# Output products of two tiles begun inside the last attention rounds, with weights, constants and last channels loaded in another order

## The chip, the cores and the metric

One core of a Trainium2 chip runs the whole program. Its engines work side by side, each on its own list of instructions in a fixed order: PE (matrix products; its weight loads are listed as PEld), DVE and ACT (elementwise work, both read PSUM), POOL (elementwise work on SBUF) and SP, which here only issues DMAs. The metric is the device time of one execution in microseconds (us), as the median of some runs.

## The reference

The reference runs two kinds of layer in turn, twice: attention over a sliding window, then a spectral filter.

```python
def _A_ref(x, wqkv, wo):
    B, S, D = x.shape                       # 1, 2048, 576
    H = 32; Dh = D // H; W = 256            # 32 heads of 18
    qkv = (x @ wqkv).reshape(B, S, 3, H, Dh).transpose(2, 0, 3, 1, 4)
    q, k, v = qkv[0], qkv[1], qkv[2]
    scores = jnp.einsum("bhqd,bhkd->bhqk", q, k) * (Dh ** -0.5)
    ...  # causal mask, window of 256
    p = _softmax(scores, axis=-1)
    o = jnp.einsum("bhqk,bhkd->bhqd", p, v)
    return o.transpose(0, 2, 1, 3).reshape(B, S, D) @ wo
...
x = x + _A_ref(_layernorm(x, axis=-1), A_wqkv, A_wo)
x = x + _B_ref(_layernorm(x, axis=-1), B_w_r, B_w_i)   # rfft2, times W, irfft2
x = x + _A_ref(_layernorm(x, axis=-1), A_wqkv, A_wo)
x = x + _B_ref(_layernorm(x, axis=-1), B_w_r, B_w_i)
```

The change lies in the last part of each attention layer: the products with `wo`, and how they join the attention that comes before.

## The kernel before

`layer_a` works through the heads in 8 groups (n) of four heads, and through the tokens in 16 blocks (i) of 128. A round `t` of its loop runs from -10 (`-LEAD`) to 129 (`NX + 1`), with `NX` = 128 pairs of group and block. In a round stand, on PE in this order, twice (for `pair` 0 and 1): two E products (`exps`: keys against queries, of pair `t`, which ACT then exponentiates into `P`), two S products (`score_max`: of pair `t + 10`, whose row maxima DVE takes), and in pair 0 also the product of probabilities and values of pair `t - 2` (`pv`, sixteen small products into the bank `U`). POOL masks the `P` tiles. S products end with round 117, so rounds 118 to 127 have E products alone. Every fourth round `m_rows` turns the maxima (`tpm`) and `norm` turns and divides a finished chunk of 512 tokens (`tpo`), and stores it to DRAM: channels 0 to 447 to `o_d`, the last 128 to `o7_d`.

PSUM has eight banks. Here they are held as three of the tag S, two of E, two of pj and the bank `U`. The function `bank` hands them out in rotation, from the list `banks`: S, S, E, E, S while projections hold pj, and with the two pj banks in the list from round 103 on. A product into a bank waits until the reader of its last content is done; so in a list of n banks it waits for the reader of the n-th use before.

The output product goes by 16 tiles of 128 tokens (u; tile u holds every sixteenth token). Its channels come back from DRAM (`load`: 448 channels into `o`, and the tile of x beside it; `last`: the last 128 channels of all tiles into `o7`), are turned by PE (`turn`, `turn_last`) and split into a high and a low part by ACT, DVE and POOL. `early` makes the products of the first 448 channels, eleven steps of two halves (288 columns each); `late` makes the three steps of the last 128 channels, adds x on DVE and stores the tile. Tiles 0 to 2 have their early products right behind the loop, between the last transposes of attention (`tpz`, whose results go into `o7` without passing through DRAM); then come the late products of tiles 0 to 2, and from tile 3 on a pipeline that the spectral layer shares. `OB` is 120. The tiles of weights, constants (`dc`, `gc`) and channels lie in SBUF where the projections' inputs were, which are free from round 103 on.

No scheduler moves anything: the order on each engine is that of the code.

Of the kernel before, what the change touches and what calls it, by code (L numbers as in the profile page):

```python
# [8 lines left out]
F32 = mybir.dt.float32  # L9
F32R = mybir.dt.float32r  # L10
# [5 lines left out]
S, D = 2048, 576  # L16
DF = 289
NF = 290
# [409 lines left out]
NQ = 8  # L428
# [72 lines left out]
class Out:  # L501


    def __init__(self, nc, ident, eps, bp, ov, o7v, srcv, dstv, wo_d, dc_d, gc_d):
        self.__dict__.update(nc=nc, ident=ident, eps=eps, bp=bp, ov=ov, o7v=o7v, srcv=srcv, dstv=dstv, wo_d=wo_d, dc_d=dc_d, gc_d=gc_d)
        self.ps = {}

# [21 lines left out]
    def consts(self):  # L529

        self.dcs = []
        for k, t in enumerate(("wraw", "wraw", "wqh", "wqh", "wql")):
            d = self.bp.tile([128, 2, NF], F32R, tag=t, name=f"dc{k}", bufs=2)
            self.nc.sync.dma_start(d.bitcast(F32), self.dc_d[:, 2 * k:2 * k + 2].bitcast(F32))
            self.dcs.append(d)
        self.nc.sync.dma_start(self.gc.rearrange("p a c -> p (a c)").bitcast(F32), self.gc_d.bitcast(F32))

    def load(self, u):
        self.nc.sync.dma_start(self.o[u % 3], self.ov[:, u])
        self.nc.sync.dma_start(self.x[u % 5], self.srcv[:, u])  # L540
# [7 lines left out]
    def turn(self, u, tp, e, last=None):  # L548
# [11 lines left out]
        if last is not None:  # L560
            self.split_last(u, last)

    def turn_last(self, u, tp):
        self.nc.tensor.transpose(tp, self.o7[:, u], self.ident)
# [6 lines left out]

    def steps(self, u, ks, first, last):
        for i, (x, p, wk) in enumerate(ks):
            for n in range(2):
                self.nc.tensor.matmul(self.ps[u][n][:, 0:288], x, self.w[p][:, wk * D + n * 288:wk * D + n * 288 + 288],  # L575
                                      start=first and i == 0, stop=last and i == len(ks) - 1)

    def early(self, u, ps, some=slice(0, 11)):
# [10 lines left out]
        self.steps(u, ks[some], some.start == 0, False)  # L589

# [38 lines left out]
def layer_a(tc, src, dst, wqk_d, wv_d, wo_d, dc_d, gc_d, dram, copy, wvs, wos, second, spectral):  # L629
# [9 lines left out]
    with ExitStack() as ctx:  # L639
# [129 lines left out]
        with ExitStack() as c2:  # L769
# [55 lines left out]

            banks, later, stores = ["S", "S", "E", "E", "S"], [], []

# [133 lines left out]

            OB = NX - 8
            out = Out(nc, ident, eps, bp, ov, o7v, srcv, dstv, wos, dc_d, gc_d)

            for t in range(-LEAD, NX + 2):
# [58 lines left out]
                if t - OB - 3 in (0, 1, 2, 4):  # L1024
                    out.tail(min(t - OB - 3, 3))
                if t - OB - 5 in (0, 1, 2):
                    u = t - OB - 5
                    out.turn(u, pp.tile([128, 512], F32, tag="pj", name=f"tpa{u}", bufs=2), V)
                    if u < 2:
                        out.load(u + 3)  # L1030
# [5 lines left out]
            for k in range(4):  # L1036
                tp = pp.tile([128, 512], F32, tag="E" if k in (1, 2) else "pj", name=f"tpz{k}", bufs=2)[0:32]
                for a in range(4):
                    T.transpose(tp[:, 128 * a:128 * a + 128], us[NQ - 1, 3][:, 4 * k + a:512:16], ident)
                tv = tp.rearrange("p (a h e) -> p a h e", a=4, h=4)  # L1040
# [6 lines left out]
            tp = pp.tile([128, 512], F32, tag="pj", name="tpl", bufs=2)  # L1047
# [15 lines left out]
            out.turn(4, pp.tile([128, 512], F32, tag="E", name="tpa4", bufs=2), A)  # L1063
        spectral(dst, out.dcs, out.gc, ident, out.rh, out.rl, out)
# [30 lines left out]
```

## Time and profile before

| | |
|---|---|
| median of 3 runs | 1461.99 us (1460.09 to 1463.79) |
| profiled execution | 1459.43 us |
| its span | 1457.7 us |
| granted PE clock, mean | 0.975 |
| PE busy | 1362.7 us (93%) |
| DVE, ACT, POOL busy | 946.6, 809.0, 710.8 us |
| L575, the output products | 784 products, 113.8 us |
| loop of the first attention layer ends, its second | 481.12, 1205.85 us |

The busy time of PE is a sum of spans in which products overlap, so a stretch of time is better read from the starts of its instructions. In the order of time a row gives start, length, engine, line, operation, what it writes and reads, the shape and how many like it were merged; behind it, in brackets, how long the engine was idle before and what ended that.

### The profile page before, as it was taken

How to read it: one execution, taken by the hardware profiler on the slowest of the kernel's cores; microseconds unless marked ns; L12 is line 12 of the kernel's file. 1: busy time of each engine (PE TensorE's matmuls, PEld its weight loads, DVE VectorE, ACT ScalarE, POOL GpSimd, SP SyncE). 2: the span in 40 equal slices, each digit the busy share in tenths (PEclk: the TensorE clock that was granted, in tenths of full speed). 3: DMA queues.
4: the chain of work that ended last, by engine and by line, in shares of the span. 5: the costliest groups of instructions: out<-in, count | busy, mean ns of one | idle time of the engine just before them, and what ended most of it. 6: DMA issues, size and time to landing. Idle time of an engine off the chain costs nothing.

```text
span 1457.7 us, 35798 instructions
## 1 busy us (share of the span) xinstructions
PE 1362.7 (93%) x12536; PEld 1063.8 (73%) x12536; DVE 946.6 (65%) x3053; ACT 809.0 (56%) x1907; POOL 710.8 (49%) x1205
## 2 busy tenths in 40 slices
PE   7998999999999999887879999999999998998888
PEld 7987666666665889847879876666666657997478
DVE  4347778887776566564543487778877864565645
ACT  5622677667768344325545236776676683443255
POOL 2345556666655333153612555655555552431536
PEclk9999999999999999997989999999999999999979
DMA  7866455545546657686575575555454565576865
GB/s 231 263 184 221 152 168 176 172 156 176 161 144 174 191 183 220 201 246 207 202 237 123 162 227 165 161 155 157 137 153 142 162 182 162 186 225 200 238 215 193
DMA packets 198335, 269.93 MB, mean 185 GB/s; under 512 B 86988, under 2 KB 109068, under 8 KB 196940
## 3 DMA queue, kind: packets, MB, share of 16 engines
q1 hardware_dynamic: 188428, 251.04, 56.1%
q10 hardware_dynamic: 9216, 13.37, 2.9%
q0 software_dynamic: 512, 3.23, 0.8%
q8 instruction: 101, 1.65, 0.5%
q14 instruction: 78, 0.64, 0.1%
HBM read 166.34 MB, written 103.79 MB: 185 GB/s over the span
## 4 chain that ended last, share of the span: by engine, by line
PE 77%; DMA 10%; DVE 5%; ACT 4%; issue 2%; POOL 1%; SPq 1%; ACTq 0%; DVEq 0%; POOLq 0%
PE pj L803 14%; PE U L919 11%; PE S L871 9%; PE E L899 9%; PE vps L759 8%; PE ops L575 6%; PE po L216 3%; PE pf L216 3%; PE pi L401 2%; PE tpo L929 2%; DMA ofree<-yd 1%; ACT P L900 1%; DMA o_d<-o 1%; DMA qs<-mt 1%; PE pz L236 1%
## 5 line engine op out<-in xcount | busy, mean ns | idle before, releaser
L873 DVE CUSTOM_DVE_ANT_0 jk<-S,mask 128x384 bf16<-128x384 f32 (+2 forms) x1024 | 497.6, 529 | 94.9 <-PE S L871 90.2
L900 ACT ACTIVATE P<-E 128x384 f32<-128x384 f32 (+2 forms) x1024 | 422.2, 477 | 172.3 <-PE E L899 142.3
L902 POOL TENSOR_SCALAR_AFFINE_SELECT P<-P 128x512 f32<-128x512 f32 x256 | 162.3, 634 | 274.3 <-ACT P L900 262.7
L871 PE MATMUL S<-ks,qs 63*128 63x384 f32 (+2 forms) x1024 | 237.8, 365 | 3.4 <-ACT P L900 1.0
L899 PE MATMUL E<-qs,ks 64*128 64x384 f32 (+2 forms) x1024 | 220.9, 395 | 7.9 <-DMA qs<-mt 5.2
L919 PE MATMUL U<-P,vq 128*19 128x128 f32 (+1 forms) x3840 | 203.1, 330 | 2.5 <-POOL P L905 2.0
L899 PEld LDWEIGHTS E<-qs,ks 64*128 64x128 f32 x1024 | 119.1, 184 | 83.8 <-issue 32.5
L871 PEld LDWEIGHTS S<-ks,qs 63*128 63x128 f32 x1024 | 132.2, 185 | 50.0 <-ACT P L900 23.0
L803 PE MATMUL pj<-xh,wqh 64*128 64x512 f32 (+1 forms) x640 | 164.8, 403 | 2.1 <-ACT vt L763 1.7
L919 PEld LDWEIGHTS U<-P,vq 128*19 128x19 f32 x3840 | 90.1, 98 | 95.7 <-issue 34.4
L905 POOL TENSOR_SCALAR_AFFINE_SELECT P<-P 128x512 f32<-128x512 f32 x224 | 142.0, 634 | 0.0
L803 PE MATMUL pj<-xl,wqh 64*128 64x512 f32 (+1 forms) x512 | 127.8, 393 | 0.0
L803 PE MATMUL pj<-xh,wql 64*128 64x512 f32 (+1 forms) x640 | 121.3, 392 | 0.0
L575 PE MATMUL ops<-oroom 128*128 128x288 f32 x784 | 113.8, 301 | 4.4 <-DVE oroom L558 3.0
L575 PEld LDWEIGHTS ops<-oroom 128*128 128x128 f32 x784 | 106.6, 191 | 6.2 <-DVE oroom L558 4.0
L803 PEld LDWEIGHTS pj<-xh,wqh 64*128 64x128 f32 (+1 forms) x640 | 87.3, 187 | 7.5 <-ACT vt L763 2.1
L185 POOL TENSOR_TENSOR eo<-xn 128x287 f32<-128x287 f32 x32 | 26.1, 816 | 124.9 <-ACT xn L183 120.0
L873 DVE DVE_READ_ACCUMULATOR2_ANT m<- 128x1 f32 x1024 | 84.7, 83 | 0.0
L803 PEld LDWEIGHTS pj<-xh,wql 64*128 64x128 f32 (+1 forms) x640 | 73.1, 186 | 7.4
L817 POOL TENSOR_TENSOR sg<-sg 128x512 fp32r<-128x512 f32 x56 | 72.0, 1286 | 4.7
L803 PEld LDWEIGHTS pj<-xl,wqh 64*128 64x128 f32 (+1 forms) x512 | 70.9, 188 | 3.8
L759 PE MATMUL vps<-wvh,xh 128*128 128x288 f32 x320 | 73.0, 310 | 0.0
(228 smaller groups left out, 2472.5 us busy)
## 6 DMA issues: line engine op xcount, KB each, us to landing
qk_d<-sg SPq DMA_DIRECT2D x56, 512.0 KB
qs<-qk_d SPq DMA_DIRECT2D x384, 72.0 KB
ks<-qk_d SPq DMA_DIRECT2D x384, 72.0 KB
v_d<-vt SPq DMA_DIRECT2D x32, 304.0 KB
vq<-v_d SPq DMA_DIRECT2D x16, 608.0 KB
wt<-in_w SPq DMA_DIRECT2D x16, 580.0 KB
x<-ofree SPq DMA_DIRECT2D x32, 288.0 KB
ofree<-x SPq DMA_DIRECT2D x16, 576.0 KB
```

The source lines that it names most:

```text
L216: T.matmul(o, et[:, c, si], m(5 * c + mi), start=q == 0, stop=False)
L575: self.nc.tensor.matmul(self.ps[u][n][:, 0:288], x, self.w[p][:, wk * D + n * 288:wk * D + n * 288 + 288], start=first and i == 0, stop=la ...
L759: T.matmul(ps[:, n, 0:288], xT(xk, c), w[:, wk, n * 288:(n + 1) * 288], start=i == 0, stop=i == len(ks) - 1)
L803: T.matmul(ps, w[r, wk], xT(xk, cs)[r], start=s == 0, stop=s == len(ks) - 1)
L817: (P if halves else V).tensor_sub(sg[:, 1], su, sg[:, 0].bitcast(F32))
L871: T.matmul(ps[:, 0:N], q[b:b + 63, pair, i * 128:i * 128 + 128], k[b:b + 63, pair, lo:hi], start=True, stop=True)
L873: V.tensor_tensor_reduce(out=jk[:, 0:N], in0=ps[:, 0:N], in1=mask[:, 384 - N:384], scale=1.0, scalar=-3e38, op0=ALU.add, op1=ALU.max, accu ...
L899: T.matmul(ps[:, 0:nq], k[b:b + 64, pair, j * 128:j * 128 + 128], q[b:b + 64, pair, j * 128:j * 128 + nq], start=True, stop=True)
L900: A.activation(p[:, hl_, 0:nq], ps[:, 0:nq], AF.Exp, scale=SC)
L902: P.affine_select(out=p[:, :, 0:128], in_=p[:, :, 0:128], pattern=[[0, 4], [1, 128]], compare_op=ALU.is_ge, fill=0.0, base=0, channel_mult ...
L905: P.affine_select(out=p[:, :, 256:384], in_=p[:, :, 256:384], pattern=[[0, 4], [-1, 128]], compare_op=ALU.is_gt, fill=0.0, base=0, channel ...
L919: T.matmul(U[32 * h:32 * h + 19, (q0 % 4) * 128:(q0 % 4) * 128 + 128 * (q1 - q0)], vts[n][:, j, h], pt[n, j][:, h, (q0 - j) * 128:(q1 - j) ...
```

## The change

- The early products of tiles 0 and 1 are made in rounds 115 to 125, two steps of two halves in each round, behind `pv` and ahead of the E products of pair 1 (`begun`). Tile 0 holds the two pj banks from round 114 on, tile 1 two of the S banks from round 118 on; the third S bank is held by one tile, F.
- So the list of banks loses pj at round 113 (it was 125), and from round 118 on is E, E, F.
- The first 384 channels of tiles 0 and 1 are loaded in rounds 111 and 112 and turned by themselves (`load_main`, `turn_main`, rounds 114 and 118); channels 384 to 447 come in rounds 116 and 117 and are turned for both tiles together (`turn_tails`, round 121).
- The weights are loaded in the order in which steps use them, the constants one a round in rounds 115 to 120 (they stood together in round 123).
- The last channels of the first 1536 tokens come in three loads, each two rounds or so behind its store, where there was one.
- Behind the loop stand tile 2's early products alone, half by half, between the `tpz` transposes; tile 3 is turned ahead of `tpl`, the transposes of the last channels.

```diff
@@ class Out
     def weights(self, k):
-        c = slice(k // 2 * D, k // 2 * D + D)
-        self.nc.sync.dma_start(self.w["hl"[k % 2]][:, c].bitcast(F32), self.wo_d[k % 2, :, c].bitcast(F32))
+        p, b = ("h0", "h1", "h2", "l0", "l1", "l2", "h4", "l4", "h3", "l3")[k]
+        c = slice(int(b) * D, int(b) * D + D)
+        self.nc.sync.dma_start(self.w[p][:, c].bitcast(F32), self.wo_d["hl".index(p), :, c].bitcast(F32))
...
+    def turn_main(self, u, tp, copy):
+        T, o, oT = self.nc.tensor, self.o[u % 3], self.oT[u % 3]
+        for kt in range(3):
+            T.transpose(tp[:, kt * 128:kt * 128 + 128], o[:, kt * 128:kt * 128 + 128], self.ident)
+        copy(oT[:, 0:384], tp[:, 0:384])
+        self.nc.vector.tensor_sub(oT[:, 512:896], tp[:, 0:384], oT[:, 0:384].bitcast(F32))
...
-    def steps(self, u, ks, first, last):
+    def steps(self, u, ks, first, last, halves=(0, 1)):
         for i, (x, p, wk) in enumerate(ks):
-            for n in range(2):
+            for n in halves:
...
@@ layer_a
+                if tag == "F":
+                    return fixed[0]
                 return pp.tile([128, 512], F32, name=name, tag=tag, bufs=3 if tag == "S" else 2)
...
+            begun = {OB - 5: [(0, 0, 2)], OB - 4: [(0, 2, 4)], OB - 3: [(0, 4, 6)], OB - 2: [(0, 6, 8)], OB - 1: [(0, 8, 9), (1, 0, 1)], OB: [(1, 1, 3)],
+                     OB + 1: [(1, 3, 5)], OB + 2: [(1, 5, 7)], OB + 3: [(0, 9, 11)], OB + 4: [(1, 7, 9)], OB + 5: [(1, 9, 11)]}
...
-                if t == OB + 5:
+                if t == OB - 7:
                     banks = [tag for tag in banks if tag != "pj"]
+                if t == NX - LEAD:
+                    first, fixed = [[pp.tile([128, 512], F32, tag="S", name=f"{k}_{n}", bufs=3) for n in range(z)] for k, z in (("ops1", 2), ("F", 1))]
+                    banks = ["E", "E", "F"]
...
+                    if pair == 0 and t in begun:
+                        for u, a, b in begun[t]:
+                            out.early(u, None, slice(a, b))
...
-                if t - OB in (0, 1, 2):
-                    out.load(t - OB)
-                if t == OB + 3:
-                    out.consts()
+                if t - OB in (-9, -8):
+                    out.load_main(t - OB + 9)
+                if t - OB in (-4, -3):
+                    out.load(t - OB + 4, slice(384, 448))
+                if t == OB - 6:
+                    out.turn_main(0, pp.tile([128, 512], F32, tag="pj", name="tpm0", bufs=2), A.copy)
+                    out.ps[0] = [pp.tile([128, 512], F32, tag="pj", name=f"ops0_{n}", bufs=2) for n in range(2)]
+                if t == NX - LEAD:
+                    out.ps[1] = first
+                    out.turn_main(1, bank("tpm1"), V.tensor_copy)
...
+                if t in range(OB - 5, OB + 1):
+                    out.consts(t - OB + 5)
+                if t == OB + 1:
                     out.last(slice(96, 128), slice(0, 56))
-                if t == NX - 1:
-                    out.last(slice(0, 96), slice(0, 128))
...
+                if t - OB in (1, 5, 7):
+                    c = (t - OB) // 3
+                    out.last(slice(32 * c, 32 * c + 32), slice(0, 128))
...
-            out.early(0, [pp.tile([128, 512], F32, tag="S", name=f"ops0_{n}", bufs=3) for n in range(2)], slice(0, 4))
+            out.early(2, [fixed[0], None], slice(0, 8), (0,))
...
-            out.early(0, None, slice(4, 11))
-            out.early(1, [pp.tile([128, 512], F32, tag=k, name=f"ops1_{k}", bufs=b) for k, b in (("S", 3), ("E", 2))])
...
+            turn_z(0, bank_e("tpz0"))
+            turn_z(1, bank_e("tpz1"))
+            turn_z(2, U)
+            out.early(2, None, slice(8, 11), (0,))
+            turn_z(3, bank_e("tpz3"))
+            out.ps[2][1] = bank_e("ops2_1")
+            out.early(2, None, slice(0, 11), (1,))
+            out.turn(3, U, A)
+            out.tail(4)
...
-            out.early(2, [pp.tile([128, 512], F32, tag=k, name=f"ops2_{k}", bufs=2) for k in ("E", "pj")])
-            out.turn(3, U, A)
-            out.tail(4)
```

Three places show how the rows move. PE in round 121 of the first layer, before (the E products are named by round and head; every one takes the next of seven banks):

```order
L899 MATMUL E121_0_8033<-qs1_1053,ks1_1054 128x384
L899 MATMUL E121_2_8036<-qs1_1053,ks1_1054 128x384
L919 MATMUL U_1055<-P7_6_7945,vq7_7111 19x256 x4
L919 MATMUL U_1055<-P7_7_7984,vq7_7111 19x128 x4
L899 MATMUL E121_1_8049<-qs1_1053,ks1_1054 128x384
L899 MATMUL E121_3_8052<-qs1_1053,ks1_1054 128x384
L899 MATMUL E122_0_8060<-qs1_1053,ks1_1054 128x384
L899 MATMUL E122_2_8063<-qs1_1053,ks1_1054 128x384
```

The same place in the change, where F is an E product too, into the bank of that name:

```order
L919 MATMUL E121_0_8090<-qs1_1053,ks1_1054 128x384
L919 MATMUL E121_2_8093<-qs1_1053,ks1_1054 128x384
L939 MATMUL U_1055<-P7_6_7980,vq7_7111 19x256 x4
L939 MATMUL U_1055<-P7_7_8029,vq7_7111 19x128 x4
L593 MATMUL ops1_0_7977<-oroom_7362 128x288
L593 MATMUL ops1_1_7978<-oroom_7362 128x288
L593 MATMUL ops1_0_7977<-oroom_7362 128x288
L593 MATMUL ops1_1_7978<-oroom_7362 128x288
L919 MATMUL F_0_7979<-qs1_1053,ks1_1054 128x384
L919 MATMUL E121_3_8112<-qs1_1053,ks1_1054 128x384
L577 MATMUL tpt_8117<-ident_77,ofree_7363 128x128 x2
L919 MATMUL F_0_7979<-qs1_1053,ks1_1054 128x384
```

Four early products of tile 1 stand between U and the next E products, F comes back three bank uses later, and the tails' transposes (`tpt`) take a turn in the rotation.

PE behind the loop, before: the end of tile 1's early products, `tpl`, and the start of tile 2's.

```order
L575 MATMUL ops1_S_8341<-oroom_7362 128x288
L575 MATMUL ops1_E_8342<-oroom_7362 128x288
L564 MATMUL tpl_8365<-ident_77,ofree_7363 128x128 x3
L575 MATMUL ops2_E_8375<-oroom_7362 128x288
L575 MATMUL ops2_pj_8376<-oroom_7362 128x288
```

In the change, from the end of the loop on:

```order
L593 MATMUL F_0_7979<-oroom_7362 128x288 x8
L1080 MATMUL tpz0_8333<-ident_77,us7_15_8323 32x128 x4
L1080 MATMUL tpz1_8341<-ident_77,us7_15_8323 32x128 x4
L1080 MATMUL U_1055<-ident_77,us7_15_8323 32x128 x4
L593 MATMUL F_0_7979<-oroom_7362 128x288 x3
L1080 MATMUL tpz3_8359<-ident_77,us7_15_8323 32x128 x4
L593 MATMUL ops2_1_8367<-oroom_7362 128x288 x11
L556 MATMUL U_1055<-ident_77,ofree_7363 128x128 x3
L557 MATMUL U_1055<-ident_77,ofree_7363 128x128
L582 MATMUL tpl_8387<-ident_77,ofree_7363 128x128 x3
L593 MATMUL ops0_0_7834<-oroom_7362 128x288
```

Tile 2's products are all ahead of `tpl`, and tile 0's late products follow it at once.

SP in the last rounds, before, from the round of the constants to the load of the last channels:

```order
L534 DMA dc0_8117<-dcr_62 128x580
L534 DMA dc1_8119<-dcr_62 128x580
L534 DMA dc2_8121<-dcr_62 128x580
L534 DMA dc3_8123<-dcr_62 128x580
L534 DMA dc4_8125<-dcr_62 128x580
L536 DMA oroom_7362<-gcr_64 128x256
L543 DMA ofree_7363<-o7_d_73 32x16x56
L539 DMA ofree_7363<-o_d_72 128x448
L540 DMA ofree_7363<-in_x 128x576
L939 DMA o7_d_73<-o7_2_8221 128x4x72
```

The change, from the last of the constants on:

```order
L537 DMA oroom_7362<-gcr_64 128x256
L547 DMA ofree_7363<-o7_d_73 32x16x56
L547 DMA ofree_7363<-o7_d_73 32x2048
L959 DMA o7_d_73<-o7_1_8155 128x4x72
L543 DMA ofree_7363<-o_d_72 128x448
L544 DMA ofree_7363<-in_x 128x576
L543 DMA ofree_7363<-o_d_72 128x448
L544 DMA ofree_7363<-in_x 128x576
L547 DMA ofree_7363<-o7_d_73 32x2048
L959 DMA o7_d_73<-o7_2_8271 128x4x72
L547 DMA ofree_7363<-o7_d_73 32x2048
```

The constants no longer stand just ahead of the last store to `o7_d`, and the load behind that store brings a third of what it brought (96x2048 before).

More of the change, by code (lines that the diff above doesn't have):

```diff
@@ L561, in turn, with turn_tails @@
             self.split_last(u, last)
+    def turn_main(self, u, tp, copy):
[4 more added lines that the diff above has]
+        self.nc.vector.tensor_sub(oT[:, 512:896], tp[:, 0:384], oT[:, 0:384].bitcast(F32))
+    def turn_tails(self, tp):
+        for u in range(2):
+            self.nc.tensor.transpose(tp[:, 128 * u:128 * u + 128], self.tl[u], self.ident)
+        self.nc.vector.tensor_copy(self.rh[:, 5760:7552].rearrange("p (k c) -> p k c", k=2)[:, :, 384:512],
+                                   tp[:, 0:256].rearrange("p (k c) -> p k c", k=2))
     def turn_last(self, u, tp):
@@ L570, in split_last, with early @@
         self.nc.vector.tensor_sub(oL[:, 128:256], tp, oL[:, 0:128].bitcast(F32))
-    def steps(self, u, ks, first, last):
+    def steps(self, u, ks, first, last, halves=(0, 1)):
         for i, (x, p, wk) in enumerate(ks):
-            for n in range(2):
+            for n in halves:
                 self.nc.tensor.matmul(self.ps[u][n][:, 0:288], x, self.w[p][:, wk * D + n * 288:wk * D + n * 288 + 288],
                                       start=first and i == 0, stop=last and i == len(ks) - 1)
-    def early(self, u, ps, some=slice(0, 11)):
+    def early(self, u, ps, some=slice(0, 11), halves=(0, 1)):
         oT = self.oT[u % 3]
@@ L588, in early @@
         ks += [(c(3), "h", 4), (c(3), "l", 4)]
-        self.steps(u, ks[some], some.start == 0, False)
+        self.steps(u, ks[some], some.start == 0, False, halves)
     def late(self, u):
@@ L824, in proj @@
                 return [lambda s=s, k=k: mm(s, k) for s, k in enumerate(ks)]
-            banks, later, stores = ["S", "S", "E", "E", "S"], [], []
+            banks, later, stores, fixed = ["S", "S", "E", "E", "S"], [], [], []
             def store():
@@ new lines, in layer_a @@
+                if t - OB in (-4, -3):
[6 more added lines that the diff above has]
+                    out.turn_main(1, bank("tpm1"), V.tensor_copy)
+                if t - OB in (-1, 0):
+                    out.tail(t - OB + 1)
@@ new lines, in layer_a @@
+                if t == OB + 1:
+                    out.turn_tails(bank("tpt"))
+                if t - OB in (0, 2, 3):
+                    out.load((2, 0, 3, 4)[t - OB])
+                if t in range(OB - 5, OB + 1):
+                    out.consts(t - OB + 5)
+                if t == OB + 1:
+                    out.last(slice(96, 128), slice(0, 56))
+                if t - OB in (1, 5, 7):
+                    c = (t - OB) // 3
+                    out.last(slice(32 * c, 32 * c + 32), slice(0, 128))
@@ L1031, in layer_a @@
+                if t - OB in (4, 6):
+                    out.tail(2 + (t - OB) // 5)
+                if t == OB + 6:
+                    out.turn(2, bank("tpa2"), V)
                 if t == NX:
                     A.activation(wp.tile([128, 1], F32, name="se", bufs=1), eps, AF.Sqrt)
-            out.early(0, [pp.tile([128, 512], F32, tag="S", name=f"ops0_{n}", bufs=3) for n in range(2)], slice(0, 4))
-            for k in range(4):
-                tp = pp.tile([128, 512], F32, tag="E" if k in (1, 2) else "pj", name=f"tpz{k}", bufs=2)[0:32]
+            out.early(2, [fixed[0], None], slice(0, 8), (0,))
@@ L1038, in layer_a, with turn_z @@
+            def turn_z(k, tp):
                 for a in range(4):
-                    T.transpose(tp[:, 128 * a:128 * a + 128], us[NQ - 1, 3][:, 4 * k + a:512:16], ident)
-                tv = tp.rearrange("p (a h e) -> p a h e", a=4, h=4)
+                    T.transpose(tp[0:32, 128 * a:128 * a + 128], us[NQ - 1, 3][:, 4 * k + a:512:16], ident)
+                tv = tp[0:32].rearrange("p (a h e) -> p a h e", a=4, h=4)
                 rc = wp.tile([128, 4, 4, 1], F32, tag="rc", name=f"rcz{k}", bufs=2)[0:32]
@@ L1062, in layer_a @@
                     out.split_last(4, tp[:, 0:128])
-            out.turn(4, pp.tile([128, 512], F32, tag="E", name="tpa4", bufs=2), A)
+            out.turn(4, pp.tile([128, 512], F32, tag="S", name="tpa4", bufs=3), A)
         spectral(dst, out.dcs, out.gc, ident, out.rh, out.rl, out)
```

29 lines of the change are left out of this document (13 added, 16 removed).

## The prediction

> **What bounds the kernel now.** I read the stretches of the first attention layer's end (its second layer repeats them 725 us later), then the order of time in single rounds, then the chain of waits behind the loop. The stretches are the last score rounds, the rounds with exponentials alone, the loop's end, and the output product until its first wait-free unit; the columns are length, busy time of PE, PEld, DVE, ACT and POOL, granted clock, DMA share and GB/s.
>
> ```profile
> 446.00:461.40 15.40, 14.96 (x164) 8.78 (x162) 14.97 (x61) 11.69 (x33) 7.38 (x12) 1.00 0.74 210
> 461.40:475.70 14.30, 13.07 (x173) 7.05 (x173) 2.77 (x9) 13.71 (x36) 9.94 (x18) 1.00 0.52 154
> 475.70:481.10 5.40, 5.40 (x82) 3.41 (x82) 3.90 (x8) 4.17 (x12) 3.69 (x9) 1.00 1.00 327
> 481.10:499.20 18.10, 15.26 (x117) 14.22 (x113) 8.29 (x29) 3.34 (x10) 1.11 (x4) 1.00 0.41 128
> ```
>
> PE looks full everywhere, but these spans overlap, so I go by starts. ACT fills 13.71 of 14.30 us of the exponential rounds: they are its own. A score round is set by something else; here is round 116, with seven PSUM banks in rotation (start, length, engine):
>
> ```profile
> 457.63 0.85 PE L919 MATMUL U<-P,vq 128*19 128x256 f32 x16
> 458.41 0.44 PE L899 MATMUL E<-qs,ks 64*128 64x384 f32 x2
> 458.89 1.26 ACT L900 ACTIVATE P<-E 128x384 f32<-128x384 f32 x3 [0.53 <-PE E L899]
> 459.10 0.77 PE L871 MATMUL S<-ks,qs 63*128 63x384 f32 x2
> 459.80 0.84 PE L919 MATMUL U<-P,vq 128*19 128x256 f32 x16
> L900 ACT ACTIVATE P<-E x1024: 272/490/632, 132.9 to 1204.1; 128x384 f32<-128x384 f32 x150, 128x128 f32<-128x128 f32 x11, 128x256 f32<-128x256 f32 x10
> ```
>
> From U to U it is 2.17 us: U takes 0.78, the E product behind it reaches ACT 0.48 later, its exponential takes 0.49 (the median in the last row), and only then, at 459.43 (459.87 less 0.44), does the second S start, into a bank seven uses back, which that exponential has just freed; 0.37 later comes U. 0.78 + 0.48 + 0.49 + 0.05 + 0.37 = 2.17. So the round is a ring through a bank, not one engine's work. Where projections hold the two pj banks, five banks rotate, and the ring is longer:
>
> ```profile
> 306.20 0.85 PE L919 MATMUL U<-P,vq 128*19 128x256 f32 x16
> 306.98 0.44 PE L899 MATMUL E<-qs,ks 64*128 64x384 f32 x2
> 307.45 0.87 ACT L900 ACTIVATE P<-E 128x384 f32<-128x384 f32 x2 [0.36 <-PE E L899]
> 308.38 0.19 PEld L871 LDWEIGHTS S<-ks,qs 63*128 63x128 f32 x2 [0.20 <-ACT P L900]
> 308.38 0.44 PE L871 MATMUL S<-ks,qs 63*128 63x384 f32 x2
> 308.75 0.72 PE L919 MATMUL U<-P,vq 128*19 128x256 f32 x9
> ```
>
> S, five uses behind, waits for the second exponential: 0.78 + 0.47 + 0.87 + 0.06 + 0.37 = 2.55 us. What stands between U and the next E lengthens such a ring by its whole length, and that is where the change puts its early products.
>
> The other rows that carry the sum, in order of time again, are starts of rounds, the normalising of a chunk, the ends of the two loops, and the splitting of the last channels:
>
> ```profile
> 461.44 0.84 PE L919 MATMUL U<-P,vq 128*19 128x256 f32 x16
> 463.60 0.85 PE L919 MATMUL U<-P,vq 128*19 128x256 f32 x16
> 468.65 0.85 PE L919 MATMUL U<-P,vq 128*19 128x256 f32 x16 [1.01 <-POOL P L905]
> 469.79 0.66 PE L929 MATMUL tpo<-ident,us 128*128 128x128 f32 x4
> 470.49 0.26 DVE L932 RECIPROCAL rc<-tpo 128x16 f32<-128x16 f32 x1 [6.40 <-PE tpo L929]
> 470.78 0.46 DVE L934 TENSOR_TENSOR o<-tpo,rc 128x288 f32<-128x288 f32 x1
> 475.70 0.84 PE L919 MATMUL U<-P,vq 128*19 128x256 f32 x16 [0.19 <-ACT us L924]
> 481.12 1.32 PE L575 MATMUL ops<-oroom 128*128 128x288 f32 x8
> 482.28 1.91 PE L1039 MATMUL tpz<-ident,us 128*32 128x128 f32 x16
> 490.12 0.27 ACT L569 CAST oroom<-tpl 128x128 fp32r<-128x128 f32 x1 [8.26 <-PE tpl L564]
> 490.42 0.29 DVE L570 TENSOR_TENSOR oroom<-tpl,oroom 128x128 fp32r<-128x128 f32 x1 [4.49 <-ACT oroom L569]
> 1205.85 1.32 PE L575 MATMUL ops<-oroom 128*128 128x288 f32 x8
> ```
>
> The chain of waits behind the loop (start, length, what; the last two rows are of the second layer):
>
> ```profile
> 478.73 5.62 DMA o_d<-o
> 484.36 5.13 DMA ofree<-o_d
> 489.54 0.55 PE tpl L564 x3
> 493.48 0.59 ACT oroom L557
> 494.57 0.81 DVE ofree L597 x2
> 499.22 3.98 PE ops L575 x28
> 1214.94 0.55 PE tpl L564 x3
> 1224.62 1.53 PE ops L575 x5
> ```
>
> U starts at 461.44 in round 118, 463.60 in 119 and 475.70 in 126; 481.12 and 1205.85 are the ends of the loops. Behind them the transpose tpl waits for a store and a reload of the last channels, 5.62 + 5.13 us.
>
> **The change part by part.** *Taken from behind the loop.* The early products of tiles 0 and 1, 44 products. Behind the loop then stand: 8 products (1.16 us by the row at 481.12), 12 of the 16 transposes (0.11 each, 1.3), 3 products (0.4), 4 transposes (0.44), 11 products (1.5) and tile 3's turn (0.6): 5.4 us until tpl, where it was 8.4 in the first layer and 9.1 in the second. Behind tpl the 22 products of tile 2 no longer cover the splitting of the last channels. Late products of tile 0 now wait for tile 3's copy and subtraction (0.59 at 493.48, then some 0.6), one copy and subtraction for tpl (490.12 to 490.71, 0.6), themselves 0.8 and 0.3 to the first addition: additions begin 2.9 us behind tpl instead of 5.0 (494.57 less 489.54). The rest, 4.65 to 499.22, is chained on DVE and stays. 5.4 + 2.9 + 4.65 = 12.95 against 18.10 and 18.77 (1224.62 less 1205.85): gains of 5.15 and 5.8, together 11.0 us. This needs the reload not to be last any more. The constants' loads leave its way (they go 3 to 8 rounds earlier) and it shrinks from 768 to 256 KB; I cost it at nothing, hidden by the 9 us of PE work between store and tpl. If it still took 10.75, tpl would come 1.7 us later in each layer.
>
> *Put into the loop.* Two steps of two halves are four products. Half of the eight at 481.12 is 0.58, and the changes of tile shape before and after add a little: I take 0.62; ends 0.54 (0.13 each, as in runs of them) and 0.70.
>
> *Banks taken away.* The pj pair leaves the rotation at round 113 rather than 125, and from round 118 two S banks hold tile 1 and three banks (E, E, F) rotate. The trace of before shows no rotation of three, so I write the ring down as in the two rounds above. The E products come as a pair, U and early, and a second pair; the second product of the next round's first pair goes into the bank of this round's third product. U 0.78, early 0.62, E to ACT 0.47, one exponential 0.49, release 0.06, E to the next U 0.37: 2.79 us a round. The bounds of it: 1.94, if only PE's work counted (E pairs and U 1.32 from 472.07 to 473.39, and 0.62), and 3.2, if a second exponential had to end first, as with five banks.
>
> ```profile
> 472.07 0.85 PE L919 MATMUL U<-P,vq 128*19 128x256 f32 x16
> 473.39 0.85 PE L919 MATMUL U<-P,vq 128*19 128x256 f32 x16
> ```
>
> Per layer: rounds 113 and 114, five banks and no early product, 2 x (2.55 - 2.17) = +0.8. Rounds 115 to 117, 3 x (2.55 + 0.62 - 2.17) = +3.0. Round 118: the normalising transposes go into F and wait for its exponential (U + 1.40 + 0.47 + 0.49 + 0.06 = 2.42), and the next round's second E waits in turn for DVE to read them, 1.45 later (469.79 to 471.24), then 0.06 and 0.37: 4.3 against 2.16, +2.1. Rounds 119 to 125: 7 x 2.79, and two rounds in which another transpose takes a bank and a second exponential must end, 2 x 0.39: 20.3 against 12.1, +8.2. Rounds 126 to 129, two more transposes in three banks: an estimate of +0.8, two waits of about 0.4 us. Sum +14.9, in two layers +29.8. Turning tiles 0 and 1 earlier moves the same transposes; the copies move to ACT and DVE, which a longer round leaves idle. POOL's splits of the tails stay inside its slack (9.94 of 14.30). The weights are issued in the same rounds in another order, the first needed ten rounds on: nothing. SP issues six loads more in each layer, about half a microsecond each, spread over rounds of nearly 3 us: nothing.
>
> Net: 29.8 - 11.0 = +18.8 us. The profiled execution took 1459.43 us (span 1457.7), which gives 1478.2; the median, 1461.99, lies 2.56 higher, so I say 1481.
>
> **Rivals.** *Banks do not bind: faster.* If E products never waited for a bank, a round would be the larger of PE and ACT work: 1.94 against the 1.73 of now in rounds 119 to 125 (+1.5), and about +0.2 in each of three score rounds (0.6): 2.1 a layer against 5.5 saved, -6.7 us, 1455. For it: DVE is busy for 2.77 of 14.30 us there, and ACT's 13.71 would pace rounds hardly longer than now. Against it: the ring reproduces two rounds to 0.01 us, where no engine has 2.17 or 2.55 us of work, and the LDWEIGHTS row at 308.38 names ACT. It decides from a round of about 2.2 us downward. The Trainium skill (Perfetto Trace Analysis, Optimization Strategy) says that interleaving stretches with different bounding engines may help, which is this rival's result; it adds that a gap repeating on the engine that should be full can mean too little PSUM for the next tile, and the 0.36 us gap on ACT at 307.45 is of that sort.
>
> *No difference:* the score rounds lengthen as said, but the exponential rounds come out near 2.0, about 5.5 us a layer each way, 1462.
>
> *The reload is still last:* +3.4 us, 1484.
>
> *The clock drops.* After a stretch in which PE has waits, the second layer shows a lower granted clock, though the first, with the same waits, shows 1.00:
>
> ```profile
> 1220.00:1225.00 5.00, 2.70 (x18) 1.99 (x17) 4.37 (x19) 1.12 (x5) 0.00 (x0) 0.97 0.42 160
> 1225.00:1230.00 5.00, 5.00 (x29) 5.00 (x29) 1.72 (x6) 2.39 (x5) 2.77 (x6) 0.69 0.60 172
> ```
>
> If short waits in each round did that at 0.7, the 1.77 us of PE's part of a ring would become 2.5 in 11 rounds, +8 a layer, 1497. The wait of 1.01 us at 468.65 did not. The Trainium skill (TensorE: Matmul & The Clock Gate, "A second HAM failure mode: psum-queue depth-cycling") tells of such gaps making the clock swing; by it 1497 is the result, and the 1.00 in the stretch 461.40:475.70 does not agree.
>
> **How the numbers follow.** The forecast 0.72, faster 0.09, no difference 0.07, reload last 0.07, clock 0.05. The forecast's own range: the early block's ends give 0.08 x 11 x 2 = 1.8 us each way, the estimates of rounds 113, 114, 118 and 126 to 129 could be nothing or half as large again (3.7 a layer: 7 down, 4 up): 1472 to 1487. With the reload and half of what lies toward no difference the range is 1468 to 1489; beyond it stay faster, no difference and clock. A change of 0.3%, 4.4 us, is about what can be told here: faster 0.09, same 0.08, slower 0.83.
>
> **What would show it.** Right: U starts 2.7 to 2.9 us apart in rounds 119 to 125, with ACT idle by over 1 us in each until an E product; LDWEIGHTS of E waiting for ACT; three score rounds near 3.2; tpl about 5.4 us behind the loop's end with no DMA named; about 13 us from the loop's end to the next units. Wrong: rounds under 2.2, with ACT still full; tpl waiting for the reload; a granted clock under 0.9 within the loop.

## The result and the profile after

| | before | after |
|---|---|---|
| median | 1462.15 us (1460.09 to 1463.79, 4 runs) | 1485.12 us (1481.03 to 1486.57, 4 runs) |
| profiled execution, its span | 1459.43, 1457.7 us | 1484.70, 1483.0 us |
| granted PE clock, mean | 0.975 | 0.974 |

The ratio is 1.0153 (95% interval 1.0129 to 1.0177): slower by 23 us. 1481 was predicted, 1468 to 1489 as the range. Of the four executions of the first kernel below, the banks alone, one took 1824.05 us at a granted clock of 0.648, against 0.966 to 0.971 in the other three; its median is that of those three.

The stretches of the changed kernel (length, busy PE, PEld, DVE, ACT, POOL, granted clock, DMA share, GB/s) are its score rounds with early products and its rounds with exponentials alone:

```profile
455.80:465.20 9.40, 8.71 (x84) 5.15 (x82) 6.33 (x24) 5.60 (x15) 2.44 (x4) 1.00 0.73 219
472.60:490.60 18.00, 16.08 (x151) 9.23 (x150) 1.14 (x3) 11.17 (x27) 8.86 (x18) 1.00 0.50 151
```

ACT, which filled 13.71 of 14.30 us in the exponential rounds, now has 11.17 of 18.00: it waits. The clock is 1.00 in both. One of these rounds in the order of time, all engines (line numbers of the changed kernel: `pv` is L939, `steps` L593, `exps` L919 and L920):

```profile
472.64 0.85 PE L939 MATMUL U<-P,vq 128*19 128x256 f32 x16
473.42 0.78 PE L593 MATMUL ops<-oroom 128*128 128x288 f32 x4
474.13 0.44 PE L919 MATMUL F<-qs,ks 64*128 64x384 f32 x1
474.61 0.49 ACT L920 ACTIVATE P<-E 128x384 f32<-128x384 f32 x1 [1.24 <-PE F L919]
475.15 0.44 PE L919 MATMUL E<-qs,ks 64*128 64x384 f32 x1 [0.41 <-ACT P L920]
475.52 0.63 PE L939 MATMUL U<-P,vq 128*19 128x256 f32 x8
```

From U to U it is 2.88 us. The early products start 0.78 behind U and take 0.71, the E pair reaches ACT 0.48 later, one exponential takes 0.49, and 0.05 behind its end the next E starts on PE, which waited 0.41 us for it; 0.37 later comes U. While the early products run, ACT has nothing: it was idle for 1.24 us. This is the ring of the prediction, in its very order.

To see what each stretch cost, here are starts in the second layer, where no transfer disturbed these rounds in either kernel. First those of before (U of rounds 112, 115, 118, 119 and 126), with U of round 112 in the first layer ahead of them:

```profile
448.94 0.84 PE L919 MATMUL U<-P,vq 128*19 128x256 f32 x16
1173.70 0.85 PE L919 MATMUL U<-P,vq 128*19 128x256 f32 x16
1180.20 0.85 PE L919 MATMUL U<-P,vq 128*19 128x256 f32 x16
1186.17 0.85 PE L919 MATMUL U<-P,vq 128*19 128x256 f32 x16
1188.33 0.85 PE L919 MATMUL U<-P,vq 128*19 128x256 f32 x16
1200.44 0.84 PE L919 MATMUL U<-P,vq 128*19 128x256 f32 x16 [0.19 <-ACT us L924]
```

and those of after: the same rounds, then the loop's end, tpl and the first unit that the spectral layer shares, with U of round 112 in the first layer, `turn_main`'s transposes and the unit there ahead of them.

```profile
447.45 0.85 PE L939 MATMUL U<-P,vq 128*19 128x256 f32 x16
454.82 0.55 PE L571 MATMUL tpm<-ident,ofree 128*128 128x128 f32 x3 [0.41 <-DMA ofree<-o_d]
508.83 3.98 PE L593 MATMUL ops<-oroom 128*128 128x288 f32 x28 [1.27 <-DVE oroom L562]
1190.27 0.85 PE L939 MATMUL U<-P,vq 128*19 128x256 f32 x16
1198.05 0.85 PE L939 MATMUL U<-P,vq 128*19 128x256 f32 x16
1207.47 0.85 PE L939 MATMUL U<-P,vq 128*19 128x256 f32 x16
1211.92 0.85 PE L939 MATMUL U<-P,vq 128*19 128x256 f32 x16
1232.82 0.85 PE L939 MATMUL U<-P,vq 128*19 128x256 f32 x16
1238.47 1.32 PE L593 MATMUL F<-oroom 128*128 128x288 f32 x8
1243.89 0.49 PE L582 MATMUL tpl<-ident,ofree 128*128 128x128 f32 x3
1251.00 1.19 PE L593 MATMUL ops<-oroom 128*128 128x288 f32 x7 [1.27 <-DVE oroom L562]
```

| second layer, us | before | after | grew by | predicted |
|---|---|---|---|---|
| U112 to U115 | 6.50 | 7.78 | 1.28 | 0.8 |
| U115 to U118 | 5.97 | 9.42 | 3.45 | 3.0 |
| U118 to U119 | 2.16 | 4.45 | 2.29 | 2.1 |
| U119 to U126 | 12.11 | 20.90 | 8.79 | 8.2 |
| U126 to the loop's end | 5.41 | 5.65 | 0.24 | 0.8 |
| loop's end to the unit | 18.77 | 12.53 | -6.24 | -5.8 |
| sum | 50.92 | 60.73 | 9.81 | 9.1 |

In the first layer the same stretch grew from 50.28 (448.94 to 499.22) to 61.38 (447.45 to 508.83), by 11.10. Together that is 20.9 of the 23 us between the medians.

### The profile page after: what moved, and what is told of

Same layout as the page of the kernel before. It is cut to its first block, busy times and chain, and to the rows that moved or that the text cites. A ratio compares the mean times of both kernels' runs of the same rounds, so it can differ in the third digit from the quotient of the medians.

```text
span 1483.0 us, 35808 instructions
## 1 busy us (share of the span) xinstructions
PE 1379.7 (93%) x12536; PEld 1066.5 (72%) x12536; DVE 946.9 (64%) x3053; ACT 815.2 (55%) x1909; POOL 712.0 (48%) x1205
## 5 line engine op out<-in xcount | busy, mean ns | idle before, releaser
L920 ACT ACTIVATE P<-E 128x384 f32<-128x384 f32 (+2 forms) x998 | 416.3, 475 | 195.3 <-PE E L919 156.3
L919 PE MATMUL E<-qs,ks 64*128 64x384 f32 (+2 forms) x998 | 228.4, 397 | 16.2 <-DMA qs<-mt 8.1
L939 PE MATMUL U<-P,vq 128*19 128x128 f32 (+1 forms) x3840 | 203.5, 330 | 0.0
L919 PEld LDWEIGHTS E<-qs,ks 64*128 64x128 f32 x998 | 122.1, 184 | 96.2 <-issue 38.1
L939 PEld LDWEIGHTS U<-P,vq 128*19 128x19 f32 x3840 | 89.8, 98 | 92.4 <-issue 36.0
L593 PE MATMUL ops<-oroom 128*128 128x288 f32 x868 | 130.6, 301 | 5.6 <-DVE oroom L562 3.0
L593 PEld LDWEIGHTS ops<-oroom 128*128 128x128 f32 x868 | 117.5, 188 | 13.0 <-issue 4.8
```

Of the source, the lines that this page charges most:

```text
L919: T.matmul(ps[:, 0:nq], k[b:b + 64, pair, j * 128:j * 128 + 128], q[b:b + 64, pair, j * 128:j * 128 + nq], start=True, stop=True)
L920: A.activation(p[:, hl_, 0:nq], ps[:, 0:nq], AF.Exp, scale=SC)
L939: T.matmul(U[32 * h:32 * h + 19, (q0 % 4) * 128:(q0 % 4) * 128 + 128 * (q1 - q0)], vts[n][:, j, h], pt[n, j][:, h, (q0 - j) * 128:(q1 - j) ...
```

## The experiments

The theory: a round is a ring through PSUM banks, and both halves of the change, fewer banks and products between U and the next E pair, lengthen it. Rivals: banks do not bind and the products' own work counts; or the ring is right but the reload or the clock takes part of the time. The first four kernels were timed against 27 runs of the kernel before (median 1462.17 us), the last three against 17 (1463.82).

**The banks alone.** The changed kernel with the early products of tiles 0 and 1 behind the loop again; banks, loads and turns as in the change.

```diff
-                    if pair == 0 and t in begun:
-                        for u, a, b in begun[t]:
-                            out.early(u, None, slice(a, b))
...
+            for u in range(2):
+                out.early(u, None)
             out.early(2, [fixed[0], None], slice(0, 8), (0,))
```

> The change with its banks (no pj from round 113, E, E, F from round 118) but all early products of tiles 0 and 1 behind the loop. Theory (a ring through a bank sets the round; with measured parts: five banks 2.55 us, three banks 2.89 - 0.72 = 2.17 us): U starts 2.55 apart in rounds 115 to 117 and 2.17 in rounds 119, 120, 123 to 125, against 1.32 to 2.4 (mean 1.73) before; loop +8.1 us a layer, the output product behind it as long as before; +16 us, about 1478. Rival (the early products' PE time inside the rounds is the cost, banks are no matter): rounds as before, mean 1.73, time within 2 us of before, 1462.

Measured: 1485.86 us (3 runs), ratio 1.0164 (1.0134 to 1.0193), as slow as the change with the 44 products back where they were. Starts in its second layer, U of rounds 115, 119 and 120, a transpose of round 121 that waits for its load, U of round 126, the loop's end and the unit:

```profile
1198.07 0.85 PE L939 MATMUL U<-P,vq 128*19 128x256 f32 x16
1209.22 0.85 PE L939 MATMUL U<-P,vq 128*19 128x256 f32 x16
1211.38 0.85 PE L939 MATMUL U<-P,vq 128*19 128x256 f32 x16
1215.44 0.33 PE L577 MATMUL tpt<-ident,ofree 128*128 128x128 f32 x1 [0.42 <-DMA ofree<-o_d]
1225.79 0.85 PE L939 MATMUL U<-P,vq 128*19 128x256 f32 x16
1231.44 6.11 PE L593 MATMUL ops<-oroom 128*128 128x288 f32 x44
1249.79 3.99 PE L593 MATMUL ops<-oroom 128*128 128x288 f32 x28 [1.27 <-DVE oroom L562]
```

From round 115 to 126 it takes 27.72 us, against 20.24 before and 34.77 in the change. So the banks, with the earlier turns, cost 7.5 us there and the products another 7.05 (0.64 for each of eleven blocks, less than their 0.71). Part of the 7.5 is not the banks': round 121, in which `tpt` waits 0.42 us for its load, takes 3.10 (U at 1213.55 and 1216.65) and round 122 takes 2.55 (to 1219.20), where in the change both take 3.26 (1217.69, 1220.95, 1224.21). Without that wait round 121 would be some 0.55 shorter, so I estimate 6.9 us for banks and turns and 7.6 for the products, 0.69 a block. A round with three banks and no early product is 2.16 (1209.22 to 1211.38): the same ring without its second link, 0.78 + 0.47 + 0.49 + 0.05 + 0.37. And from the loop's end to the unit it is 18.35 us, 5.82 more than in the change. Moving the products costs 7.05 and earns 5.82, a loss even with the banks already taken. (No kernel here takes the banks without turning tiles 0 and 1 earlier, so the two share their price.)

Its total is over the 1478 of the ring. In the trace the excess lies in the first layer, where the clock fell twice behind late loads. The first time is behind a wait of `turn_main` for its load, the second in rounds 121 to 123. Here are that first wait and the stretch of the second:

```profile
456.73 0.90 PE L571 MATMUL tpm<-ident,ofree 128*128 128x128 f32 x3 [0.90 <-DMA ofree<-o_d]
474.60:484.70 10.10, 9.27 (x67) 4.30 (x66) 1.14 (x3) 5.72 (x15) 4.17 (x8) 0.66 0.41 112
```

and in the order of time the transpose of round 121, which waits for its load here too, and the U behind it:

```profile
476.54 0.33 PE L577 MATMUL tpt<-ident,ofree 128*128 128x128 f32 x1 [0.42 <-DMA ofree<-o_d]
478.00 1.49 PE L939 MATMUL U<-P,vq 128*19 128x256 f32 x16
```

U takes 1.49 us instead of 0.85; behind the same wait in the second layer the next U takes 0.85. From U112 to the unit this kernel needs 64.30 us in the first layer (448.86 to 513.16) and 59.50 in the second; of the 4.8 between them 2.5 lie ahead of round 118 and 2.3 in rounds 121 to 125. So the price of banks and turns is read from the second layer: 59.50 against 50.92 before, +8.6 us, about 8.0 without the wait of round 121, of the change's 9.8. In the loop they cost 2.7 us from U112 to U118 (1190.29 to 1205.49), with five banks, and 6.0 from there to U126, with three.

**The same products at the round's end.** The changed kernel with the early products behind the second E pair instead of ahead of it: same work, same banks.

```diff
-                    if pair == 0 and t in begun:
+                    if pair == 1 and t in begun:
```

> The change with the early products half a round later, behind the second pair of E products instead of ahead of it; the same products, banks and loads. Theory (ring): there they stand in the 1.02 us in which PE waits for an exponential to free a bank, so rounds 119, 120, 123 to 125 fall from 2.89 to 2.2 to 2.3 us and rounds 115 to 117 from 3.27 to 2.6; about 17 us less than the change, 1467 to 1470, still slower than before because of the banks. Rival (PE work added to a round is what counts): rounds stay at 2.9 and 3.2, time as the change, 1485.

Measured: 1470.9 us (8 runs), ratio 1.006 (1.0039 to 1.0081). One place in the order is worth 14 us, where the theory had some 17. An exponential round in its first layer, and in its second U of rounds 115 and 126, the loop's end and the unit:

```profile
469.31 0.85 PE L939 MATMUL U<-P,vq 128*19 128x256 f32 x16
470.09 0.43 PE L919 MATMUL E<-qs,ks 64*128 64x384 f32 x1
470.46 0.79 PE L593 MATMUL ops<-oroom 128*128 128x288 f32 x4
471.18 0.45 PE L919 MATMUL E<-qs,ks 64*128 64x384 f32 x2
471.56 0.85 PE L939 MATMUL U<-P,vq 128*19 128x256 f32 x16
1188.16 0.85 PE L939 MATMUL U<-P,vq 128*19 128x256 f32 x16
1216.39 0.85 PE L939 MATMUL U<-P,vq 128*19 128x256 f32 x16
1222.05 1.32 PE L593 MATMUL F<-oroom 128*128 128x288 f32 x8
1234.58 3.99 PE L593 MATMUL ops<-oroom 128*128 128x288 f32 x28 [1.27 <-DVE oroom L562]
```

The round is 2.25: U 0.78, a pair 0.37, the early products 0.72, a pair 0.38, back to back. The products now run while ACT works on the pairs, and PE's own work, a little over the ring's 2.16, ends last. From 115 to 126 it is 28.23 us, 0.5 more than with the banks alone, or 1.1 more than these without the wait of round 121; no load is waited for in round 121 here. So the eleven blocks, 7.05 us in the change (7.6 by the estimate), are mostly hidden. The score rounds fell less than expected: rounds 115 to 117 are 2.79, 2.59 and 2.42, where 2.6 was said. The unit comes 12.53 behind the loop's end, as in the change. What is left of the loss is mostly the price of banks and turns.

**Tile 0 alone, five banks kept.** The kernel before with the change's loads of constants and last channels, tile 0's early products in rounds 120 to 127 (one or two steps each, in the pj pair, which leaves the list at round 118), and five banks for the rest; tile 4 is turned in U.

```diff
+            begun = {OB: (0, 2), OB + 1: (2, 3), OB + 2: (3, 5), OB + 3: (5, 6), OB + 4: (6, 8), OB + 5: (8, 9), OB + 6: (9, 10), OB + 7: (10, 11)}
...
-                if t == OB + 5:
+                if t == NX - LEAD:
...
+                    if pair == 0 and t in begun:
+                        out.early(0, None, slice(*begun[t]))
```

> Before, with tile 0 alone begun in the loop, in rounds 120 to 127 (one or two steps a round) when no scores are left; pj leaves the rotation at round 118, five banks remain, none for tile 1; tile 4 is turned in U; constants and last channels are loaded as in the change. Theory: with five banks and E products alone the ring (E to the fifth use behind) is shorter than the round, so rounds are set by ACT or PE work, 1.7 to 2.0 us: loop +1 us a layer; loop's end to the end of tile 4's turn 14.5 us instead of 18.1 and 18.8: -6 us, about 1456. Rival 1 (any loss of banks stalls the loop as three do): rounds over 2.3, +5 us a layer, about 1465. Rival 2 (the reload of the last channels stays last, 10.7 us behind its store): tpl at 8.3 us behind the loop, no gain, 1461 to 1464.

Measured: 1464.33 us (12 runs), ratio 1.001 (0.9994 to 1.0025): no gain that can be told, and my 1456 was missed. One of the rounds in order, then the loop's end and the unit:

```profile
476.62 0.85 PE L919 MATMUL U<-P,vq 128*19 128x256 f32 x16
477.40 0.78 PE L575 MATMUL ops<-oroom 128*128 128x288 f32 x4
478.66 0.85 PE L919 MATMUL U<-P,vq 128*19 128x256 f32 x16
487.19 1.32 PE L575 MATMUL ops<-oroom 128*128 128x288 f32 x8
501.05 2.12 PE L575 MATMUL ops<-oroom 128*128 128x288 f32 x14 [1.49 <-DVE oroom L558]
```

The tail did what was expected, 13.86 us in place of 18.10, and no product waits for a bank in that round. But it is 2.04 long where before it was 1.32 (472.07 to 473.39), longer by the 0.72 of its early products; from U of round 120 to the loop's end it is 19.66 us against 16.19 (464.93 to 481.12), and from U112 the whole loop grew by 5.3. I had priced a round with early products at 1.7 to 2.0, on the idea that ACT sets the pace and PE has room. In the round shown PE has none: with the banks that are left, its own work comes last. The time is that of rival 1, 1465 with +5 us a layer, but not for its reason: of the 5.3 us, 3.5 lie behind U of round 120, where the 22 products are, and only between U of rounds 117 and 118 does a product wait for a bank (460.95 to 463.26, 2.31 us against 1.64 before).

**The loads alone.** The kernel before with the constants one a round and the last channels in three loads.

```diff
-                if t == OB + 3:
-                    out.consts()
+                if t in range(OB - 5, OB + 1):
+                    out.consts(t - OB + 5)
...
-                if t == NX - 1:
-                    out.last(slice(0, 96), slice(0, 128))
+                if t - OB in (1, 5, 7):
+                    c = (t - OB) // 3
+                    out.last(slice(32 * c, 32 * c + 32), slice(0, 128))
```

> Before, with only the constants' loads (one a round in rounds 115 to 120) and the three loads of the last channels of the change. Theory: tpl's waits for the reload (0.56 and 1.23 us) vanish, the store takes 2 to 3 us instead of 5.6 and 6.4; -1.8 us, 1460; rounds unchanged. Rival: the constants delay the transfer of the maxima (qs<-mt) of round 118, E products of round 122 wait for it, up to +2 us a layer, 1464.

Measured: 1461.64 us (12 runs), ratio 0.9998 (0.9984 to 1.0013). In its first layer the loop, which also starts some 3 us later, ends at 484.51, and tpl and the unit follow:

```profile
492.21 0.49 PE L564 MATMUL tpl<-ident,ofree 128*128 128x128 f32 x3
501.83 3.98 PE L575 MATMUL ops<-oroom 128*128 128x288 f32 x28 [1.27 <-DVE oroom L558]
```

The wait for the reload is gone: tpl comes 7.70 behind the loop's end, not 8.42, and the last store took 2.56 us until the reload was issued (481.66 to 484.22), not 5.62. The rounds are unchanged, against the rival: from U112 to the loop's end 32.49 and 32.15 us in the two layers, 32.18 and 32.15 before. The tail is 17.3 us in both layers instead of 18.10 and 18.77, some 2 us less in all; the total doesn't resolve it (the interval reaches from -2.3 to +1.9 us).

**The change with the old loads.** Constants at round 123 and the last channels in one load, as before; all else as in the change.

```diff
-                if t in range(OB - 5, OB + 1):
-                    out.consts(t - OB + 5)
...
+                if t == OB + 3:
+                    for k in range(6):
+                        out.consts(k)
...
-                if t - OB in (1, 5, 7):
-                    c = (t - OB) // 3
-                    out.last(slice(32 * c, 32 * c + 32), slice(0, 128))
+                if t == NX - 1:
+                    out.last(slice(0, 96), slice(0, 128))
```

> The change with the loads of before for constants (all in round 123) and last channels (one reload in round 127). Theory A (the reload is hidden by the 9 us of PE work behind its store, as the prediction costed it, and three loads earn nothing here since rounds are long): tpl 5.4 us behind the loop's end with no DMA named, time as the change, 1485. Theory B (store and reload still take 5.6 + 5.1 us as before): tpl waits some 2 us in each layer, 1489.

Measured: 1484.12 us (4 runs), ratio 1.0144 (1.0118 to 1.0169). The loop's end and tpl in its second layer:

```profile
1236.82 1.32 PE L593 MATMUL F<-oroom 128*128 128x288 f32 x8
1242.23 0.49 PE L582 MATMUL tpl<-ident,ofree 128*128 128x128 f32 x3
```

5.41 us apart with no DMA named, as in the change (1238.47 to 1243.89). In its first layer the reload was issued 2.13 us behind the store (494.46 and 496.59), where it took 5.62 before, and the constants' loads began 8.6 us ahead of that store instead of 5.9 (485.87; 472.86 before). That the longer rounds, by this distance, made the store shorter is argued and not shown; but in the change the three loads earn nothing.

**The loads, and tile 4 turned earlier.** The loads-only kernel with tile 4's transposes and split moved from behind the late products to ahead of tile 2's, in the bank U, so that the next unit doesn't wait for the split.

```diff
+                if u == 2:
+                    out.turn(4, U, A)
...
-            out.turn(4, pp.tile([128, 512], F32, tag="E", name="tpa4", bufs=2), A)
```

> Before, with the loads of e4 and tile 4 turned in the bank U ahead of tile 2's late products instead of in an E bank behind them. Theory: tpl's waits go (0.56 and 1.23 us), and the wait of 0.54 us for a bank and of 1.27 us for the turn's subtraction ahead of tile 3's products shrink to under 0.5 together: about 1 us a layer; in the trace 18.1 and 18.8 us from the loop's end to the next unit become 16.4; -4 us, 1458. Rival: additions of tile 2 on DVE, 498.16 in the trace of before, set the end, and the turn only moves ahead of them: -2 us, 1460, as the loads alone.

Measured: 1458.74 us (12 runs), ratio 0.9971 (0.9957 to 0.9984): the fastest of the kernels here, and faster than before by 0.29%, or 2 to 6 us. The loop's end and the unit in its first layer:

```profile
480.43 1.32 PE L575 MATMUL ops<-oroom 128*128 128x288 f32 x8
497.52 3.95 PE L575 MATMUL ops<-oroom 128*128 128x288 f32 x28 [1.79 <-DVE ofree L610]
```

17.09 us, and 17.09 in the second layer (1208.20 to 1225.29), where 16.4 was expected and the loads alone had 17.3. The unit no longer waits for its split but for a reciprocal on DVE (L610, at 497.33), which stands behind the additions of tile 2 (L597, the last at 496.92). So the time came out as the theory's 1458, but the tail did as its rival said. The two tails are 2.7 us shorter than in the first profile of before, 0.5 of it by the turn and the rest by the loads; 2.7 is within the interval, and what is left of the 5 us between the medians lies outside the stretches read here.

**The kernel before, profiled once more**, to see how far its own stretches vary.

> Before, profiled once more. In the profiles so far the E products of round 0 of the second layer waited for the row maxima's transfer 2.0 us before, 4.8 in the change and 2.3 to 3.3 in four kernels that don't differ there. If that is chance, a second profile of before shows 2 to 5 us there, and the second layer's rounds 2 to 5 lie up to 5 us later against the first profile; if it is the change's doing, 2.0 again.

Measured: 1464.15 us (one run). The first E products of its second layer (round 0):

```profile
869.82 0.44 PE L899 MATMUL E<-qs,ks 64*128 64x384 f32 x2 [2.82 <-DMA qs<-mt]
```

The same row in the first profile of before, then in after:

```profile
867.11 0.44 PE L899 MATMUL E<-qs,ks 64*128 64x384 f32 x2 [1.98 <-DMA qs<-mt]
```

```profile
881.25 0.69 PE L919 MATMUL E<-qs,ks 64*128 64x384 f32 x2 [4.82 <-DMA qs<-mt]
```

and the stretch behind it in after:

```profile
881.00:888.50 7.50, 7.25 (x43) 4.47 (x45) 3.14 (x13) 3.08 (x8) 1.23 (x2) 0.55 0.57 198
```

The wait in round 0 is 1.98 and 2.82 in two profiles of the same kernel, and 4.82 in after, where the clock then fell to 0.55 for some 7 us (over as long it was 1.00 and 0.77 in the two profiles of before). The change touches nothing in that round, and the two kernels that share its instructions there, the banks alone and the products at the round's end, waited 3.03 and 2.25. The tail varies too: from the loop's end to the unit it is 17.88 and 19.31 us in this profile, where the first had 18.10 and 18.77.

## Why the prediction was right, point by point

- **The ring with three banks** was right: 2.88 us in rounds with nothing else, against 2.79, and 2.16 without early products. The five-bank 2.55 also came back, in rounds 115 and 116 of the banks-alone kernel (1198.07, 1200.62, 1203.17). That it is a ring, and not an amount of work, is shown by the kernel with the products at the round's end: the same work and banks, 2.25.
- **The early block was the term mis-sized most**: taken as 0.62, half a run of eight and a little, with 0.70 as its upper end; it measured 0.71. Over eleven rounds and two layers that is 2.0 us; the seven blocks of rounds 119 to 125 make up the 0.6 by which that term was short (8.79 for 8.2). That 1481 came as near as it did is partly luck: in the second layer the first four rows of the table were forecast too small, by 1.7 us together, and the last two made up 1.0 of it.
- **Rounds 115 to 117** lasted 9.42 us, as predicted (9.51). Two errors cancelled: the rounds are 3.27, 3.27 and 2.88, not 3.17 each. The base was wrong as well: I took 2.17 for each, but the last of them took 1.64 before, so the growth was 3.45, not 3.0.
- **Rounds 113 and 114** grew by 0.90 (4.33 to 5.23), about the 0.8 of the sum; that the round ahead of them grows by 0.38 as well was left out. In the first layer came 0.41 us in which `turn_main` waited for its load, a new wait that I had not named.
- **Round 118** came to 4.45 for 4.3. Rounds 126 to 129 cost 0.24, not 0.8.
- **Behind the loop** the working held: tpl 5.41 and 5.42 behind its end (5.4), with no DMA named; the unit after 12.52 and 12.53, 0.4 less than my 12.95.
- **The reload as last** did not come: tpl names no DMA in the change, nor in the change with the old loads. **Banks do not bind** is refuted by the banks alone: with no early product in the loop, +8.6 us in the second layer, about 8.0 without a load's wait. **The clock** stayed at 1.00 in the changed rounds (472.60:490.60), where PE waits 0.41 or 0.47 us in four of six rounds and 0.21 in a fifth; but in the first layer of the banks-alone kernel it fell to 0.66 behind a wait of 0.42, and in that of the change with the old loads to 0.71 (455.00:460.00) behind one of 0.35, both for a load. So this rival was unlikely rather than impossible. The Trainium skill (TensorE: Matmul & The Clock Gate, "A second HAM failure mode: psum-queue depth-cycling") tells of short gaps between groups of products that make the clock swing. The rounds of the change, with such gaps in five of six and a clock of 1.00, do not agree.
- **What stays open**: 2 of the 23 us between the medians, and 4.4 of the 25.3 between the two profiled executions, lie outside the stretches that the change touches. In the traces the wait in round 0 of the second layer is 2.84 us longer, and from its row to U112 it takes 2.43 us longer (309.02 against 306.59), with the low clock; these cover the latter. Since that wait varies in the kernel before, and was shorter in two kernels that share the change's instructions there, I take it for scatter; why it was 4.82 in after and 4.89 in the change with the old loads stays open.

## What to carry to other kernels

Before work is put into a loop, write its round down as a ring: which instruction waits for which reader of which bank. Work placed inside the ring's path lengthened a round by its whole length here (2.16 to 2.88 us); the same work placed where the ring waits cost about a seventh (1.1 for 7.6 us, by the estimate above). And count the banks that the work holds for itself as a price of their own: here, with the turns that go with them, they cost about 8 us a layer with no product moved, and what the products then cost in the loop and earned behind it nearly cancelled.

## What the runs showed of the hardware

- Four products between products of other shapes take 0.71 us (473.42 to 474.13), where half of a run of eight takes 0.58. The change of shape before and after is a likely reason, but no run here tries it by itself.
- The granted clock can fall for several microseconds behind a wait as short as 0.42 us (0.66 in 474.60:484.70 of the banks-alone kernel), and stay at 1.00 behind the same wait of 0.42 in the second layer of the same kernel (1213.00:1223.00), or through six rounds of the change of which four hold one of 0.41 or 0.47 (472.60:490.60). What tells them apart no run here shows.
- The wait for one transfer, that of the row maxima at the start of a layer, went from 1.98 to 2.82 us between two executions of the same kernel; with changes elsewhere it was 2.25 to 4.89.
